# Early heads' x split straight from PSUM, decoding steps moved to other chunks, and the next decoder made ahead of its first step

## The chip, the cores and the metric

The kernel runs on one core of one Trainium2 chip. The time is the device time of one execution in microseconds (us). Kernels are compared by the median of several executions. The engines are TensorE (PE, with its weight loads PEld), VectorE (DVE), ScalarE (ACT), GpSimd (POOL) and SyncE (SP), whose queue issues all DMA transfers of this kernel.

## What is computed

Three stages follow each other: attention with a decay over 4 batches of 8 heads (sequence 576, head width 64), and two feed-forward layers on the 2304 tokens. [...]

```
def _attn_ref(q, k, v, f):                  # (4, 8, 576, 64) each, f (4, 8, 576)
    scores = scale * np.matmul(q, k.transpose(0, 1, 3, 2))
    cum = np.cumsum(np.log(np.clip(f, 0.0001, 1.0)), axis=-1)
    scores = np.where(causal, -1e9, scores + cum[..., :, None] - cum[..., None, :])
    attn = softmax(scores)
    return np.matmul(attn, v)

def _moe_ref(x, w1, w2, w3, w_out):         # x (2304, 512), d_ff 1024
    return ((x @ w1) * (x @ w2) @ w3) @ w_out

def _moe2_ref(x, w_in, w_out, a, b):        # d_ff 2048
    h = x @ w_in
    g = (a0 + a1*h + a2*h*h + a3*h*h*h) / (1 + |b0|*|h| + |b1|*h*h + 1e-6)
    return g @ w_out
```

## The kernel before

Products in the feed-forward layers keep 32-bit accuracy by splitting an operand into a high part (rounded to the matmul's 32-bit format, `...h`) and a low part (the rest, `...l`): high times high, high times low and low times high are three matmuls into one bank.

**The attention loop.** The loop over `t` walks through heads: `n, c = divmod(t, 5)`, so a head `n` has five chunks `c` of up to 128 query rows. There are 32 heads. In chunk `c` of head `n` TensorE transposes the probabilities of the head before (`p_transpose`), makes the scores of the next chunk (`score_mm`, into two banks `ps_s` used in turn), and DVE takes their maximum (`score_max`, line 328), ACT the exponential (`score_exp`, line 339), DVE the reciprocal of the sums (`score_rcp`, lines 347 and 349) and POOL multiplies by it (`score_norm`, line 354). The normalization comes in groups: for heads 0 to 7 in the chunks 3 and 0, from head 8 on in the chunks 2, 4 and 0. Everything is written out in this order by hand, and each engine works its own queue in order.

**Early heads.** Heads 0 to 7 (`n < N32`) multiply by V in plain 32-bit format (`pv_early`, into the bank pair `ps_w`, chunks 2 to 4 of the head after). Two chunks after the last of these, in chunk 0 of head `n + 2`, `pv_out` copies the result of head `n` on DVE from `ps_w` into half of `xr` (line 412); for every second head `x_split` then rounds the pair of heads on ACT into `xh` (line 423) and subtracts on DVE into `xl` (line 425, both inputs in SBUF). Heads from 8 on have `pv` into `ps_v` with split operands, `pv_out` adds two halves (ACT line 414, DVE line 415), and `x_split` subtracts on POOL.

**Loading the next pair of heads.** In an even head the transposes of the next pair's q (chunk 1) and k (end of chunk 2) go into `ps_v` (`qk_transpose`, lines 250 and 251). The transposes of q wait for `pv_out` to have read `ps_v`, those of k for `prep` to have read it (ACT line 258, DVE line 260, in chunks 2 and 3).

**Fillers.** From head 9, chunk 2, TensorE has filler work between the pieces of attention: `gen_ab` multiplies a finished batch by w1 and w2 into the banks `ps_f`, so many ns per chunk (`FILL1`). ACT copies one product to `a_sb` (line 490) and DVE multiplies (line 493). The first filler needs `xh` and `xl` of all of batch 0.

**Decoding.** A `Decoder` turns 64-bit weights into 32 bits, one `step` at a time, four jobs deep: a step's instructions are the low part of job k-3 (line 89, DVE and POOL in turn for w1 and w2), the high part of k-2 (ACT, line 92), an integer add of k-1 (POOL, line 98), shift and mask of job k (DVE, lines 102 and 105) and its low word (ACT, line 108). The transfers are issued ahead on SP (line 68). `gen_w12` has 16 jobs of 512 elements (19 steps); it is followed by `gen_wo2`, which decodes w_out of the second layer in pieces of 256 elements. `side_step` does one step; the loop calls it at the `t` of

```
    DEC_AT = {4, 10, 16, 22, 28, 34, 40}
    ...
        if t == 65:
            while side:
                side_step()
            side.append(gen_wo2())
            side_step()
        if t in DEC_AT or (46 <= t < 65 and t % 2 == 0) or (t > 65 and c in (1, 3)):
            side_step()
```

so at t = 65 (head 13, chunk 0) the last steps of the first decoder, the making of the second one with its transfers, and the second one's first step stand directly behind each other. In the chunk this place lies behind `score_max` and ahead of `prep`, `score_norm` and `pv_out`.

After the attention loop come the rest of `gen_ab`, the product of w3 and w_out, the first layer's second half and the second layer; the change touches none of them.

Of the kernel before, what the change touches and what calls it, by code (L numbers as in the profile page):

```python
# [19 lines left out]
P = 128  # L20
# [100 lines left out]
def kernel(  # L121
# [265 lines left out]
    def pv_early(n, c):  # L387
        r, v = QN[c], vf[(n // 2) % 2]
        for k in range(c + 1):
            t = ptf[:, k, Q0[c] - P : Q0[c] - P + r] if c else ptf0[n % 2]  # L390
            mm(w_ps[0:D, Q0[c] : Q0[c] + r], v[:, k, n % 2, :], t, k == 0, k == c)
# [14 lines left out]
    def pv_out(n):  # L406
        b, h = divmod(n, H)
        hp, j = divmod(h, 2)
        x = xr[hp % 2]
        a, c = slice(64 * j, 64 * (j + 1)), slice(64 * (1 - j), 64 * (2 - j))  # L410
        if n < N32:
            nc.vector.tensor_copy(x[a], w_ps[0:D])
            return
        nc.scalar.copy(xtmp[a], v_ps[c])
        nc.vector.tensor_tensor(out=x[a], in0=v_ps[a], in1=xtmp[a], op=ALU.add)

    def x_split(n):
# [6 lines left out]
        eng = nc.vector if n < N32 else nc.gpsimd  # L424
        eng.tensor_tensor(
# [31 lines left out]
    def gen_wo2():  # L457
# [5 lines left out]
        with pool("d3", "right") as rp:  # L463
            dec_ = Decoder(nc, rp, "d3", PIECE2, 3, 3, jobs)
            while dec_.step():
                yield
# [89 lines left out]
    DEC_AT = {4, 10, 16, 22, 28, 34, 40}  # L556
    FILL1 = [1300.0, 1450.0, 1350.0, 1150.0, 700.0]
    late_x = None
# [3 lines left out]
    for t in range(NCH * (NH + 1) + 2):  # L562
# [25 lines left out]
        if live:  # L588
            score_max(n, c, 0)
        if grp:  # L590
            score_rcp(grp[1], grp[2], 0)
# [9 lines left out]
        if t == 65:  # L601
            while side:
                side_step()
            side.append(gen_wo2())
            side_step()
        if t in DEC_AT or (46 <= t < 65 and t % 2 == 0) or (t > 65 and c in (1, 3)):
            side_step()
# [19 lines left out]
        if c == 0 and 0 <= n - 2 < NH:  # L627
            pv_out(n - 2)
            if n - 1 == N32:
                psw.close()  # L630
                psf = ps1.enter_context(
                    tc.tile_pool(name="psf", bufs=1, space=PSUM, reuse_waits="tile")
                )
                ps_f += [psf.tile([P, 512], F32, name=f"ps_f{i}") for i in range(2)]
        if c == 1 and n % 2 == 1 and 0 <= n - 2 < NH and n not in (H + 3, H + 5):
            x_split(n - 2)
        if n == H + 5 and c == 0:
            x_split(H + 1)
        if n == H + 5 and c == 3:
# [350 lines left out]
```

## Time and profile before

| | |
|---|---|
| median of 3 executions | 1031.2 us (1029.83 to 1032.1) |
| the profiled execution | 1027.81 us, its span 1026.0 us |
| PE busy | 985.7 us, 96% of the span |
| PEld busy | 898.1 us, 88% |
| DVE busy | 794.6 us, 77% |
| ACT busy | 673.9 us, 66% |
| POOL busy | 383.3 us, 37% |

The span is what lies between the first and the last instruction; the 1.8 us beside it are the execution's own. An engine is busy while one of its instructions is being carried out, and for PE the ends of the matmuls are modelled. In the timeline a row shows the start, the duration, the engine, the line, the operation with output and inputs, and in square brackets how long the engine sat idle ahead of it and what ended that wait. [...]

### The profile page before, as it was taken

To read this page: it belongs to the slowest core of one execution; us is meant where nothing else is said; L and a number is where in the kernel's file an instruction comes from. 1 tells how busy PE (TensorE), PEld (TensorE's weight loads), DVE (VectorE), ACT (ScalarE), POOL (GpSimd) and SP (SyncE) were. 2 spreads that over 40 slices of the span, in tenths; PEclk is the share of its full clock that TensorE was granted. 3 is DMA by queue.
4 is the path that set the end of the run, shared out by engine and by line. 5 is a ranking of instruction groups with operands and counts; after the bars stand their busy time and mean duration, and the time that the engine had idled before them with its cause. 6 is when DMAs were issued, how large, how long until landed. Compare 5 with 4: busy or idle time off the path is not lost.

```text
span 1026.0 us, 18623 instructions
## 1 busy us (share of the span) xinstructions
PE 985.7 (96%) x6224; PEld 898.1 (88%) x6224; DVE 794.6 (77%) x1799; ACT 673.9 (66%) x1542; POOL 383.3 (37%) x476
## 2 busy tenths in 40 slices
PE   6888888999999999999999999999999999999998
PEld 4666788999999999998899998899999888899997
DVE  5787886777777765788988637888888888888886
ACT  5666665666666664445566537777777777777775
POOL 7445565444444432453455401222222222222221
PEclk9999998999999999999999999999999999999999
DMA  5868465666666530665579741010010100100000
GB/s 130 216 161 180 132 154 153 179 176 178 177 180 180 152 81 30 205 204 182 178 225 302 232 139 37 1 32 32 1 62 1 31 32 1 32 32 1 32 1 32
DMA packets 126352, 114.98 MB, mean 112 GB/s; under 512 B 65456, under 2 KB 94640, under 8 KB 126256
## 3 DMA queue, kind: packets, MB, share of 16 engines
q1 hardware_dynamic: 126256, 113.79, 39.6%
q8 instruction: 49, 0.80, 0.3%
q14 instruction: 47, 0.39, 0.1%
HBM read 70.61 MB, written 23.22 MB: 91 GB/s over the span
## 4 chain that ended last, share of the span: by engine, by line
PE 84%; DVE 4%; DMA 2%; issue 2%; ACT 2%; SPq 0%; POOL 0%; DVEq 0%; POOLq 0%; ACTq 0%
PE bank L160 47%; PE ps_f L160 19%; PE ps_v L160 6%; PE ps_s L160 5%; PE ps_x L359 4%; PE ps_v L250 1%; PE ps_w L160 1%; DVE pr L328 1%; DVE d_f L102 1%; DMA d_r<-in_moe_w_in_dram 1%; PE ps_v L251 0%; DMA z_dr<-z_sb 0%; DMA d_r<-in_moe_w_dram 0%; DVE cl L433 0%; DMA d_r<-in_moe_w_out_dram 0%
## 5 line engine op out<-in xcount | busy, mean ns | idle before, releaser
L887 POOL TENSOR_TENSOR gl<-pp,gh 128x384 fp32r<-128x384 f32 x96 | 97.7, 1017 | 320.8 <-PE bank L160 267.0
L354 POOL TENSOR_SCALAR pr<-pr,st 128x128 f32<-128x128 f32 (+4 forms) x160 | 93.9, 598 | 176.2 <-DVE st L349 66.2
L328 DVE CUSTOM_DVE_ANT_0 pr<-ps_s,mask 128x128 f32<-128x128 f32 (+4 forms) x160 | 83.0, 522 | 68.3 <-PE ps_s L160 63.5
L160 PE MATMUL bank<-ch,wih 128*128 128x384 f32 x384 | 129.1, 336 | 2.0 <-DVE pp L908 2.0
L160 PE MATMUL bank<-ch,wil 128*128 128x384 f32 x384 | 129.4, 337 | 0.0
L160 PE MATMUL bank<-cl,wih 128*128 128x384 f32 x384 | 128.6, 335 | 0.0
L339 ACT ACTIVATE pr<-pr,st 128x128 f32<-128x128 f32 (+4 forms) x160 | 97.1, 607 | 32.2 <-DVE st L328 31.8
L160 PE MATMUL bank<-wo2h,gl 128*128 128x512 f32 x288 | 113.9, 395 | 0.0
L160 PE MATMUL bank<-wo2h,gh 128*128 128x512 f32 x288 | 113.5, 394 | 0.0
L160 PE MATMUL bank<-wo2l,gh 128*128 128x512 f32 x288 | 113.5, 394 | 0.0
L98 POOL TENSOR_TENSOR d_f<-d_f,d_r 128x256 int32<-128x256 int32 (+1 forms) x96 | 87.8, 915 | 45.1 <-DVE d_f L105 18.6
L894 ACT ACTIVATE h<-bank 128x384 f32<-128x384 f32 x96 | 47.0, 490 | 86.9 <-PE bank L160 86.1
L383 ACT CAST pth<-ps_x 128x256 fp32r<-128x256 f32 (+1 forms) x96 | 44.4, 462 | 61.2 <-PE ps_x L359 40.5
L160 PE MATMUL ps_s<-kh,qs 128*128 128x128 f32 (+2 forms) x192 | 76.0, 396 | 8.6 <-DVE st L328 5.2
L160 PE MATMUL bank<-cl,w3oh 128*128 128x256 f32 x288 | 80.8, 281 | 0.9 <-DVE cl L433 0.9
L160 PE MATMUL bank<-ch,w3ol 128*128 128x256 f32 x288 | 80.7, 280 | 0.5 <-DVE w3ol L777 0.5
L359 PE MATMUL ps_x<-ident,pr 128*128 128x128 f32 (+1 forms) x480 | 75.7, 267 | 5.5 <-POOL pr L354 2.8
L160 PE MATMUL bank<-ch,w3oh 128*128 128x256 f32 x288 | 80.6, 280 | 0.0
L160 PEld LDWEIGHTS bank<-ch,wih 128*128 128x128 f32 x384 | 72.0, 188 | 6.9 <-DVE pp L908 2.7
L911 DVE SCALAR_TENSOR_TENSOR qv<-qv,rr 128x384 f32<-128x384 f32 x96 | 53.7, 559 | 31.3 <-ACT rr L906 31.3
L108 ACT ACTIVATE d_r<-d_r 128x256 int32<-128x256 uint32 (+1 forms) x128 | 59.9, 471 | 26.7 <-DMA d_r<-in_moe_w_dram 13.8
L901 DVE SCALAR_TENSOR_TENSOR qv<-h,pb_abs,qv 128x384 f32<-128x384 f32 x96 | 59.1, 616 | 23.1 <-ACT qv L895 23.1
(167 smaller groups left out, 3053.6 us busy)
## 6 DMA issues: line engine op xcount, KB each, us to landing
d_r<-in_moe_w_out_dram SPq DMA_DIRECT2D x48, 256.0 KB
c_dr<-c_sb SPq DMA_DIRECT2D x64, 144.0 KB
cl<-c_dr SPq DMA_DIRECT2D x36, 256.0 KB
d_r<-in_moe_w_dram SPq DMA_DIRECT2D x16, 512.0 KB
d_r<-in_moe_w_dram SPq DMA_DIRECT2D x32, 256.0 KB
d_r<-in_moe_w_in_dram SPq DMA_DIRECT2D x32, 256.0 KB
kh<-kh SPq DMA_DIRECT2D x45, 144.0 KB
z_dr<-z_sb SPq DMA_DIRECT2D x36, 128.0 KB
```

The lines of the kernel that those rows point to most:

```text
L98: nc.gpsimd.tensor_tensor(out=u, in0=u, in1=r[:, :, 0], op=ALU.add)
L108: nc.scalar.activation(low, low.bitcast(U32), AF.Copy, scale=2.0**-29)
L160: nc.tensor.matmul(o, lhsT, rhs, start=start, stop=stop)
L328: nc.vector.tensor_tensor_reduce(out=pr[0:r, OFF[c] + a : OFF[c] + b], in0=ps_s[(t + part) % 2][0:r, 0 : b - a], in1=mask[0:r, 512 - Q0[c] ...
L339: nc.scalar.activation(x, x, AF.Exp, bias=st[0:r, 0, c : c + 1], scale=-1.0, accum_out=st[0:r, 1, c : c + 1],)
L354: nc.gpsimd.tensor_scalar(x, x, st[0:r, 1, c : c + 1], 1.0, op0=ALU.mult, op1=ALU.mult)
L359: nc.tensor.transpose(ps_x[x][:, r * j : r * (j + 1)], pr[0:r, o + P * j : o + P * (j + 1)], ident[0:r, 0:r],)
L383: nc.scalar.copy(hi, src)
L887: nc.gpsimd.tensor_tensor(out=at(gl, j), in0=at(pp, j), in1=raw(at(gh, j)), op=ALU.subtract)
L894: nc.scalar.activation(at(h2, i), h, AF.Square)
L901: nc.vector.scalar_tensor_tensor(out=at(qv, i), in0=at(h2, i), scalar=pb_abs[:, 1:2], in1=at(qv, i), op0=ALU.mult, op1=ALU.add,)
L911: nc.vector.scalar_tensor_tensor(out=at(qv, i), in0=at(qv, i), scalar=QC, in1=at(rr, i), op0=ALU.add, op1=ALU.mult)
```

## The change

Four things are changed.

- `pv_early` writes the rows of `ps_w` that belong to the head's half (0 to 63 or 64 to 127). `pv_out` rounds them for early heads on ACT straight into `xh`, and a new function `x_low` subtracts on DVE, from PSUM, into `xl`, in chunk 1 of head `n + 2`, directly behind that chunk's `score_max`. `xr`, the copy on DVE and the early heads' `x_split` fall away.
- The decoding steps of `gen_w12` stand at other `t`: 7, 12, 17, ... 42 (all chunk 2), 44, 46, 48 and then chunks 1 and 3 up to 68.
- `gen_wo2` yields once behind its making, so that it is made at t = 69 (head 13, chunk 4) and takes its first step at t = 71.
- `x_split` for heads 8 and 9 moves from t = 65 to t = 69, for heads 10 and 11 from head 13 to head 14, chunk 3. The banks `ps_f` are taken over a chunk later.

```diff
--- before.py
+++ after.py
@@ -388,7 +388,7 @@
         r, v = QN[c], vf[(n // 2) % 2]
         for k in range(c + 1):
             t = ptf[:, k, Q0[c] - P : Q0[c] - P + r] if c else ptf0[n % 2]
-            mm(w_ps[0:D, Q0[c] : Q0[c] + r], v[:, k, n % 2, :], t, k == 0, k == c)
+            mm(w_ps[HALF[n % 2], Q0[c] : Q0[c] + r], v[:, k, n % 2, :], t, k == 0, k == c)
 
     def pv(n):
         i, j = (n // 2) % 2, n % 2
@@ -409,10 +409,17 @@
         x = xr[hp % 2]
         a, c = slice(64 * j, 64 * (j + 1)), slice(64 * (1 - j), 64 * (2 - j))
         if n < N32:
-            nc.vector.tensor_copy(x[a], w_ps[0:D])
+            nc.scalar.copy(xh[0][a, hp], w_ps[a])
             return
         nc.scalar.copy(xtmp[a], v_ps[c])
         nc.vector.tensor_tensor(out=x[a], in0=v_ps[a], in1=xtmp[a], op=ALU.add)
+
+    def x_low(n):
+        hp, j = divmod(n % H, 2)
+        r = HALF[j]
+        nc.vector.tensor_tensor(
+            out=xl[0][r, hp], in0=w_ps[r], in1=raw(xh[0][r, hp]), op=ALU.subtract
+        )
 
     def x_split(n):
         b, h = divmod(n, H)
@@ -421,8 +428,7 @@
             side_step()
         x = xr[hp % 2]
         nc.scalar.copy(xh[b % 2][:, hp], x)
-        eng = nc.vector if n < N32 else nc.gpsimd
-        eng.tensor_tensor(
+        nc.gpsimd.tensor_tensor(
             out=xl[b % 2][:, hp], in0=x, in1=raw(xh[b % 2][:, hp]), op=ALU.subtract
         )
 
@@ -462,6 +468,7 @@
                 jobs.append((w_out2[P * j : P * (j + 1), cs], None, None, None, wo2_dr[j, :, cs]))
         with pool("d3", "right") as rp:
             dec_ = Decoder(nc, rp, "d3", PIECE2, 3, 3, jobs)
+            yield
             while dec_.step():
                 yield
 
@@ -553,8 +560,9 @@
     nc.gpsimd.memset(st, 1.0)
 
     NPAIR = NH // 2
-    DEC_AT = {4, 10, 16, 22, 28, 34, 40}
+    DEC_AT = {*range(7, 43, 5), 44, 46, 48, 51, 53, 56, 58, 61, 63, 66, 68}
     FILL1 = [1300.0, 1450.0, 1350.0, 1150.0, 700.0]
+    T_X1 = NCH * (H + 5) + 4
     late_x = None
     pt = []
     late = ExitStack()
@@ -587,6 +595,8 @@
             score_exp((c - 1) % NCH)
         if live:
             score_max(n, c, 0)
+        if c == 1 and 0 <= n - 2 < N32:
+            x_low(n - 2)
         if grp:
             score_rcp(grp[1], grp[2], 0)
         if late_x is not None:
@@ -598,12 +608,11 @@
         flush()
         if t == 10:
             w12["dec"].ahead = 4
-        if t == 65:
-            while side:
-                side_step()
+        if t == T_X1:
+            x_split(H + 1)
             side.append(gen_wo2())
             side_step()
-        if t in DEC_AT or (46 <= t < 65 and t % 2 == 0) or (t > 65 and c in (1, 3)):
+        if t in DEC_AT or (t > T_X1 and c in (1, 3)):
             side_step()
         if t == 0:
             first_q(1)
@@ -626,17 +635,15 @@
             late_x = (m, cc)
         if c == 0 and 0 <= n - 2 < NH:
             pv_out(n - 2)
-            if n - 1 == N32:
-                psw.close()
-                psf = ps1.enter_context(
-                    tc.tile_pool(name="psf", bufs=1, space=PSUM, reuse_waits="tile")
-                )
-                ps_f += [psf.tile([P, 512], F32, name=f"ps_f{i}") for i in range(2)]
-        if c == 1 and n % 2 == 1 and 0 <= n - 2 < NH and n not in (H + 3, H + 5):
+        if c == 1 and n - 1 == N32:
+            psw.close()
+            psf = ps1.enter_context(
+                tc.tile_pool(name="psf", bufs=1, space=PSUM, reuse_waits="tile")
+            )
+            ps_f += [psf.tile([P, 512], F32, name=f"ps_f{i}") for i in range(2)]
+        if c == 1 and n % 2 == 1 and N32 <= n - 2 < NH and n not in (H + 3, H + 5):
             x_split(n - 2)
-        if n == H + 5 and c == 0:
-            x_split(H + 1)
-        if n == H + 5 and c == 3:
+        if n == H + 6 and c == 3:
             x_split(H + 3)
         if c == 4 and n % 2 == 0 and N32 <= n < NH:
             split_v(p)
```

The order in which the instructions stand shows this at three places. On DVE, in head 2, chunks 0 to 2 (`ps_w` holds the result of head 0, `xr_136` the copied half, `xl_101` the low part, `d_f` and `d_r` the decoder's tiles, `ps_s` the scores, `ps_v` the next pair's q). Before:

```order
L349 RECIPROCAL st<-st 128x2
L102 TENSOR_SCALAR d_f_170<-d_r_166 128x512
L105 SCALAR_TENSOR_TENSOR d_f_170<-d_r_166,d_f_170 128x512
L412 COPY xr_136<-ps_w 64x576
L328 ISA pr,st<-ps_s_84,mask 128x256
L328 ISA st 128x1
L328 ISA pr,st<-ps_s_83,mask 128x384
L328 ISA st 128x1
L260 SCALAR_TENSOR_TENSOR qs_113<-ps_v,qs_112 128x576
```

and in the changed kernel:

```order
L349 RECIPROCAL st<-st 128x2
L328 ISA pr,st<-ps_s_84,mask 128x256
L328 ISA st 128x1
L420 TENSOR_TENSOR xl_101<-ps_w,xh_100 64x576
L328 ISA pr,st<-ps_s_83,mask 128x384
L328 ISA st 128x1
L102 TENSOR_SCALAR d_f_170<-d_r_166 128x512
L105 SCALAR_TENSOR_TENSOR d_f_170<-d_r_166,d_f_170 128x512
L260 SCALAR_TENSOR_TENSOR qs_113<-ps_v,qs_112 128x576
```

The decoding step moved from ahead of the maximum of chunk 1 to between the maximum of chunk 2 and `prep` of q (line 260). On DVE, in head 10, chunks 0 and 1, where line 415 is what the transposes of q wait for (`c_sb` is a filler's product). Before:

```order
L349 RECIPROCAL st<-st 128x1
L493 TENSOR_TENSOR c_sb_104<-ps_f_1072,a_sb_102 128x288
L89 TENSOR_TENSOR w2l<-d_f_171,w2h 128x2x256
L102 TENSOR_SCALAR d_f_170<-d_r_166 128x512
L105 SCALAR_TENSOR_TENSOR d_f_170<-d_r_166,d_f_170 128x512
L415 TENSOR_TENSOR xr_136<-ps_v,xtmp 64x576
L328 ISA pr,st<-ps_s_84,mask 128x256
```

and in the changed kernel:

```order
L349 RECIPROCAL st<-st 128x1
L500 TENSOR_TENSOR c_sb_104<-ps_f_1107,a_sb_102 128x288
L415 TENSOR_TENSOR xr_136<-ps_v,xtmp 64x576
L328 ISA pr,st<-ps_s_84,mask 128x256
L328 ISA st 128x1
L385 TENSOR_TENSOR ptl<-ps_x_85,pth 128x2x128
L89 TENSOR_TENSOR w1l<-d_f_169,w1h 128x2x256
L102 TENSOR_SCALAR d_f_172<-d_r_168 128x512
L105 SCALAR_TENSOR_TENSOR d_f_172<-d_r_168,d_f_172 128x512
```

The step's three instructions moved from ahead of line 415 to behind the maximum of chunk 1. On ACT, in head 13, chunk 0, around the second decoder's first low word (`d_r_1707`, a tile that a transfer of w_out fills). Before:

```order
L339 ACTIVATE pr,st<-pr,st 64x576
L92 CAST w2h<-d_f_172 128x2x256
L108 ACTIVATE d_r_1707<-d_r_1707 128x256
L383 CAST pth<-ps_x_86 128x2x128
L414 COPY xtmp<-ps_v 64x576
L423 CAST xh_1702<-xr_136 128x576
L339 ACTIVATE pr,st<-pr,st 128x128
L490 COPY a_sb_103<-ps_f_1071 128x288
```

and in the changed kernel, from head 13, chunk 4, to head 14, chunk 1 (`d_r_1808` is the same tile of the second decoder):

```order
L339 ACTIVATE pr,st<-pr,st 128x512
L430 CAST xh_1801<-xr_136 128x576
L383 CAST pt0h_133<-ps_x_86 128x128
L339 ACTIVATE pr,st<-pr,st 64x576
L383 CAST pth<-ps_x_85 128x2x128
L414 COPY xtmp<-ps_v 64x576
L339 ACTIVATE pr,st<-pr,st 128x128
L497 COPY a_sb_103<-ps_f_1106 128x288
L108 ACTIVATE d_r_1808<-d_r_1808 128x256
```

The first low word moved two chunks behind the making of its decoder, and in head 13, chunk 0, nothing that a transfer fills stands ahead of the filler's copy any more.

## Rows read from the trace of the kernel before

**Rows 1.** Busy time by stretch: start:end, length, each engine's busy us (instructions), PEclk, DMA.
```profile
18.00:97.00 79.00, 67.31 (x504) 52.11 (x504) 58.90 (x177) 51.96 (x141) 35.59 (x56) 1.00 0.77 180
97.00:171.00 74.00, 61.37 (x404) 56.20 (x403) 60.17 (x156) 45.60 (x116) 44.20 (x47) 0.91 0.60 156
171.00:400.00 229.00, 229.00 (x1699) 216.89 (x1698) 160.19 (x555) 149.91 (x398) 102.01 (x142) 1.00 0.58 152
105.70:109.00 3.30, 3.30 (x16) 3.24 (x15) 3.27 (x4) 1.77 (x6) 2.64 (x2) 0.50 0.19 41
146.60:150.00 3.40, 3.40 (x16) 3.29 (x16) 1.93 (x5) 1.45 (x4) 2.06 (x3) 0.50 0.08 26
163.70:170.40 6.70, 5.54 (x23) 5.05 (x24) 6.31 (x17) 4.09 (x13) 3.69 (x5) 0.50 0.46 126
```

**Rows 2.** Timeline of PE from 97 to 171 us: start, duration, instruction, idle ahead.
```profile
103.64 0.40 PE L160 MATMUL ps_f<-xl,w1h 128*128 128x288 f32 x1 [1.54 <-DVE xl L425]
...
116.97 0.65 PE L250 MATMUL ps_v<-ident,q_raw 128*128 128x128 f32 x4 [2.73 <-DVE xr L415]
...
145.27 0.66 PE L250 MATMUL ps_v<-ident,q_raw 128*128 128x128 f32 x4 [1.60 <-DVE xr L415]
...
164.86 0.61 PE L160 MATMUL ps_f<-xh,w1h 128*128 128x288 f32 x1 [3.44 <-ACT a_sb L490]
```

**Rows 3.** Timeline of ACT in head 13, chunk 0.
```profile
162.08 0.44 ACT L108 ACTIVATE d_r<-d_r 128x256 int32<-128x256 uint32 x1 [5.18 <-DMA d_r<-in_moe_w_out_dram]
```

**Rows 4.** Timeline of DVE and PE in head 16, chunks 1 and 2, and head 18, chunk 2.
```profile
203.22 0.28 DVE L102 TENSOR_SCALAR d_f<-d_r 128x256 int32<-128x256 int32 x1
203.53 0.43 DVE L105 SCALAR_TENSOR_TENSOR d_f<-d_r,d_f 128x256 int32<-128x256 int32 x1
...
205.45 0.75 DVE L260 SCALAR_TENSOR_TENSOR qs<-ps_v,qs 128x576 fp32r<-128x576 f32 x1
...
207.62 0.60 PE L250 MATMUL ps_v<-ident,k_raw 128*128 128x128 f32 x4
...
230.41 0.75 DVE L260 SCALAR_TENSOR_TENSOR qs<-ps_v,qs 128x576 fp32r<-128x576 f32 x1
```

**Rows 5.** Timeline of DVE in head 4, chunk 2, with a decoding step.
```profile
51.37 2.04 DVE L89 TENSOR_TENSOR w1l<-d_f,w1h 128x512 fp32r<-128x512 f32 x1
...
54.41 0.75 DVE L260 SCALAR_TENSOR_TENSOR qs<-ps_v,qs 128x576 fp32r<-128x576 f32 x1
```

**Rows 6.** Timeline of POOL at the same place.
```profile
51.55 1.30 POOL L98 TENSOR_TENSOR d_f<-d_f,d_r 128x512 int32<-128x512 int32 x1
```

**Rows 7.** Timeline of PE in the early heads: the waits for DVE.
```profile
33.72 0.50 PE L160 MATMUL ps_s<-kh,qs 128*128 128x512 f32 x1 [0.82 <-DVE st L328]
...
46.05 0.45 PE L160 MATMUL ps_s<-kh,qs 128*64 128x512 f32 x1 [1.10 <-DVE st L328]
...
55.21 0.66 PE L250 MATMUL ps_v<-ident,k_raw 128*128 128x128 f32 x4 [1.64 <-DVE qs L260]
...
65.58 0.45 PE L160 MATMUL ps_s<-kh,qs 128*64 128x512 f32 x1 [1.27 <-DVE st L328]
...
79.72 0.44 PE L160 MATMUL ps_s<-kh,qs 128*128 128x384 f32 x1 [0.63 <-DVE st L328]
...
90.61 0.50 PE L160 MATMUL ps_s<-kh,qs 128*128 128x512 f32 x1 [0.89 <-DVE st L328]
```

**Rows 8.** Instructions by line: count, duration in ns (min/median/max), first and last start, form.
```profile
L412 DVE COPY xr<-ps_w x8: 729/746/751, 32.6 to 98.0; 64x576 f32<-64x576 f32 x8
...
L425 POOL TENSOR_TENSOR xl<-xr,xh x12: 1415/1428/1435, 164.3 to 409.7; 128x576 fp32r<-128x576 f32 x12
L425 DVE TENSOR_TENSOR xl<-xr,xh x4: 750/754/3189, 44.8 to 102.8; 128x576 fp32r<-128x576 f32 x4
...
L415 DVE TENSOR_TENSOR xr<-ps_v,xtmp x23: 740/751/764, 116.2 to 399.1; 64x576 f32<-64x576 f32 x23
...
L414 ACT COPY xtmp<-ps_v x24: 631/636/639, 112.6 to 407.5; 64x576 f32<-64x576 f32 x24
```

## The prediction

> **What bounds the kernel now.** I read the busy time by stretch first, to see where TensorE (PE) is not the bound. From 171 us to 400 us PE is busy for the whole 229.00 us at the full clock, so nothing that the other engines do there can save time; after that the change alters nothing. Ahead of it are two stretches with room [rows 1]. In the early heads, 18 to 97 us, PE is busy 67.31 of 79.00 us, 11.69 us idle, with the clock at 1.00 throughout. In heads 9 to 13, 97 to 171 us, fillers are there to keep PE busy, and still 12.63 us are idle and the granted clock is 0.91: three stretches at 0.50 (1.2 GHz) hold 3.30, 3.40 and 5.54 us of busy PE [rows 1]. Work that takes x at half clock takes about x/2 at full clock, so these cost (3.30 + 3.40 + 5.54) / 2 = 6.1 us. All that the change can give is therefore 11.7 us of idle in the early heads, 12.6 us in heads 9 to 13, and 6.1 us of clock.
>
> Next I read the timeline of PE for what ended its waits. Four waits make 9.31 of the 12.63 us in heads 9 to 13: 1.54 us for the last low part of x, 2.73 and 1.60 us for `pv_out` (line 415) ahead of the transposes of q in heads 10 and 12, and 3.44 us for a filler's copy on ACT [rows 2]. The last one has its reason on ACT: in head 13, chunk 0, it stood still for 5.18 us for the first transfer of the second decoder, with that copy queued behind [rows 3]. In the early heads, six waits of 0.63 to 1.64 us end with a DVE instruction [rows 7]; five of them are a score matmul waiting for its bank.
>
> **The change part by part.** *The second decoder.* The first low word now stands two chunks behind the transfers that it needs; ACT's wait was 5.18 us and two chunks last about as long (`prep` of q came at 205.45 us in head 16 and at 230.41 us in head 18 [rows 4], ten chunks in 24.96 us, 2.5 us each), so the wait is hidden, apart from a tenth or so of it. The 3.44 us go, and with them the stretch at half clock that begins at the end of that wait (2.8 us). What is late next is head 14: `x_split` of heads 8 and 9 now runs on POOL (1.43 us [rows 8]) one chunk ahead of `pv_out` of head 12, which overwrites the same `xr` and so has to wait for it on DVE, with the maxima queued behind it and PE's transposes of q waiting for it. That costs between 0 and 1.4 us. I take 0.4, near the lower end, since a chunk lies between. Steps of the second decoder that come later lie in the stretch in which PE is never idle.
>
> *The first filler.* The 1.54 us for the low part of x go: `x_low` of head 7 stands ahead of the decoding step on DVE, not behind it, and the ACT rounding is done a chunk earlier. The later take-over of the banks `ps_f` costs nothing, since the first filler comes a chunk later still.
>
> *Steps of heads 10 and 12.* They move from chunks 0, 2 and 4 to chunks 1 and 3, so `pv_out` no longer stands behind three decoding instructions: the 2.73 and 1.60 us go. What is late next is `prep` of q in chunk 2, for which the transposes of k wait. In head 16, where steps already stand in chunks 1 and 3, `prep` ended at 206.20 us and PE came at 207.62 us, a slack of 1.42 us, with a step of 203.22 to 203.96, 0.74 us, ahead of it [rows 4]. The steps moved here are of 512 elements; the one in head 4 kept DVE from 51.37 to 54.41, 3.04 us [rows 5]. So the new wait is at most 3.04 - 0.74 - 1.42 = 0.9 us and at least none; I take 0.5 in each of the two heads, the middle, as half of the steps have no DVE subtraction. Together 2.73 + 1.60 - 1.0 = 3.3 us.
>
> *The clock.* The falls at 105.7 and 146.6 us come behind the waits of 1.54 and 1.60 us, the third one behind the 3.44 us [rows 1, 2]. With these waits gone I expect none of the three: 6.1 us.
>
> Sum of heads 9 to 13: 1.54 + 3.44 + 3.3 - 0.4 + 6.1 = 14.0 us. Its ends are 8.9 us (1.54 + 3.44 + 4.33 - 1.8 - 1.4, and the third fall alone, 2.8) and 18.7 us (all of 12.63 and 6.1).
>
> *Early heads, x.* DVE loses eight copies (0.75 us each) and four subtractions, one of which lasted 3.19 us against a median of 0.75, and gains eight of `x_low`; line 415 is of the same kind, with one input in PSUM, and lasted 0.740 to 0.764 us in 23 instances [rows 8]. ACT loses four casts and gains eight of about 0.64 us (line 414 [rows 8]); it is not what PE waits for here, so I put this at nothing, between 0 and the 8 x 0.64 us. [...]
>
> The two halves of `ps_w` buy nothing: the changed kernel's first `pv_early` matmul of a head waits for the `x_low` just made, of the other half, because the bank is tracked as one. It has been read behind the maximum of chunk 1, and a score matmul stands in front on PE, so I count this wait as hidden, too; its upper bound is 0.75 us per head.
>
> *Early heads, steps.* Moving the steps takes away five waits: 0.82 + 1.10 + 1.27 + 0.63 + 0.89 = 4.7 us [rows 7]. But four of the new places, in heads 2, 4, 6 and 8, lie directly ahead of `prep` of q, and the kernel before has one step there, in head 4. It cost PE 1.64 us [rows 7]: DVE's subtraction took 2.04 us from 51.37 us on, with POOL's add of the same step, 1.30 us, beginning at 51.55 us [rows 5, 6]. It is the step's own add that held it, in a chunk without a group of normalization, so the new places do not keep DVE from being held. I take 1.64 us for heads 6 and 8 and 1.2 for head 2, whose step has no subtraction, so 4.5 us; the wait in head 4 stays. In the odd heads the step lies ahead of the maximum of chunk 3; bounds are 0 and the 1.27 us of the wait behind the long subtraction [rows 7], and I take 0.5 for three of them, as PE has the rest of `pv_early` to do meanwhile. The early heads then lose 4.5 + 1.5 - 4.7 = 1.3 us, between a gain of 4.7 and a loss of 4.5 + 3.8 - 4.7 = 3.6.
>
> [...]
>
> **How the numbers follow.** 14.0 - 1.3 = 12.7 us. The profiled execution took 1027.81 us, so it would be 1015.1; it was 3.4 us quicker than the median of the runs, 1031.2, and I set the sum against that: 1018.5 us. A measurement can tell about 0.2%, 2 us, from no change. The base case has a chance of 0.53.
>
> **Rivals.** *More (0.14).* The five smaller waits of heads 9 to 13, 12.63 - 9.31 = 3.3 us, are DVE being late behind decoding and go as steps get rarer (two per head for three); the 1.0 and 0.4 us do not appear, and the early heads come out 2 us better than even: 14.0 + 3.3 + 1.4 + 2.0 = 20.7, so 1010.5 us.
>
> *DVE becomes the bound (0.16).* It was already busy 60.17 of 74.00 us there [rows 1], and steps held by POOL stay long. Heads 10 and 12 wait the full 0.9 us (0.8 more), two of the three falls remain (3.3), and each of five heads loses 0.7 us elsewhere (3.5): 12.7 - 7.6 = 5.1, so 1026.1 us. For it speaks that hardly a fifth of DVE's time is free; against it, that head 11 already has its steps in chunks 1 and 3 and none of the four large waits.
>
> *The second decoder does not come early enough (0.06).* SP issues in order, and if a store ahead holds its transfers, the 3.44 and 2.8 us stay: 1024.7 us. Against it speaks that they were issued and landed within the 5.18 us.
>
> *Slower (0.06): the early heads lose the clock.* They keep PE just 85% busy, and two falls came behind waits no longer than the 1.64 us that would now come four times. Each stretch of 3.4 us at half clock costs 1.7 us; eight of them are 13.6, and eight full waits for `x_low` 6.0: 12.7 - 19.6, so 1038 us. It decides from the point where both exceed 14.7 us, for instance six falls with six waits. Against it speaks that the clock stayed at 1.00 through the one wait of 1.64 us.
>
> *No change (0.05):* the two middle rivals together, 1029 to 1033 us.
>
> Faster by more than 0.2%: 0.53 + 0.14 + 0.16 + 0.06 = 0.89; within it 0.05; slower 0.06. The range, 1009.5 to 1027, spans the base case but for its ends and most of the first three rivals.
>
> **What would show it.** PE's idle time from 97 us to the end of head 13 should fall from 12.6 to about 5 us and the clock there be 1.00; no wait of ACT for a transfer of w_out above 1 us. The early heads should show waits for line 260 of 1.2 to 1.7 us in heads 2, 4, 6 and 8, and no wait of `pv_early` for `x_low` above 0.2 us. The forecast is wrong if the falls of the clock come elsewhere, or if PE's idle time in the early heads moves by more than 4 us.

## The result and the profile after

| | before | after |
|---|---|---|
| median, measured side by side | 1031.38 us (1029.83 to 1032.1) | 1018.28 us (1016.53 to 1018.97) |
| the profiled execution, its span | 1027.81 us, 1026.0 us | 1016.53 us, 1014.7 us |

The changed kernel takes 0.9879 of the time before, 95% interval 0.9863 to 0.9896: 13.1 us less between the medians, 11.3 us less between the two profiled executions. The forecast was 1018.5 us, in a range of 1009.5 to 1027.

Where the time came from is read best between three moments that both kernels have: the start of the first exponential (line 339, 128x128) of heads 9, 10 and 14. Before, these stand at 97.6, 113.1 and 176.8 us; after, at 102.5, 115.4 and 166.5 us. The busy time between these moments follows, for the kernel before and then for the changed one; columns as in [rows 1]. PEclk is the clock granted to PE as a share of full speed: in the kernel before, the fillers' matmuls of 288 columns start 0.13 us apart at 1.00 (171.27 to 172.19 us) and 0.24 us apart at 0.50 (105.74 to 107.90 us). The first spacing is 0.55 of the second, where the prediction takes x/2; the second is 1.2 columns per ns, the nearest that the traces come to the prediction's 1.2 GHz, from which nothing is worked out.

```profile
18.00:97.60 79.60, 67.81 (x506) 52.40 (x505) 59.28 (x181) 52.56 (x143) 36.20 (x57) 1.00 0.77 180
97.60:113.10 15.50, 12.05 (x74) 10.94 (x75) 13.71 (x35) 9.64 (x25) 10.05 (x12) 0.89 0.70 175
113.10:176.80 63.70, 54.62 (x371) 50.66 (x370) 49.20 (x133) 38.90 (x98) 36.53 (x39) 0.92 0.56 146
```

```profile
18.00:102.50 84.50, 70.82 (x510) 55.13 (x510) 62.51 (x187) 58.39 (x153) 41.71 (x61) 0.96 0.70 178
102.50:115.40 12.90, 9.88 (x72) 8.89 (x71) 11.53 (x28) 8.17 (x21) 7.41 (x10) 1.00 0.95 230
115.40:166.50 51.10, 49.99 (x372) 47.16 (x370) 40.07 (x122) 36.20 (x93) 28.62 (x34) 1.00 0.58 150
171.00:400.00 229.00, 229.00 (x1703) 217.38 (x1702) 159.32 (x543) 148.10 (x391) 101.77 (x140) 1.00 0.57 153
```

The same 371 and 372 matmuls of heads 10 to 13 take 51.1 us instead of 63.7: PE idles 1.1 us instead of 9.1, at full clock instead of 0.92. That is 12.6 us. Up to the start of head 10 the changed kernel is 2.3 us late; up to head 9 even 4.9, of which 1.9 us are idle time and 3.0 us busy time, for its two stretches at half clock now lie ahead of head 9 where the first one used to lie behind it. From 171 us on PE is busy throughout in both [rows 1].

The waits of PE that are left in the early heads, and the two stretches at half clock:

```profile
35.70 0.66 PE L250 MATMUL ps_v<-ident,k_raw 128*128 128x128 f32 x4 [1.49 <-DVE qs L260]
48.96 0.30 PE L160 MATMUL ps_s<-kh,qs 128*128 128x128 f32 x1 [1.47 <-DMA kh<-kh]
55.33 0.66 PE L250 MATMUL ps_v<-ident,k_raw 128*128 128x128 f32 x4 [1.63 <-DVE qs L260]
67.09 0.33 PE L359 MATMUL ps_x<-ident,pr 128*128 128x128 f32 x1 [1.03 <-POOL pr L354]
74.55 0.66 PE L250 MATMUL ps_v<-ident,k_raw 128*128 128x128 f32 x4 [1.43 <-DVE qs L260]
87.64 0.33 PE L359 MATMUL ps_x<-ident,pr 128*128 128x128 f32 x1 [1.03 <-POOL pr L354]
95.35 0.66 PE L250 MATMUL ps_v<-ident,k_raw 128*128 128x128 f32 x4 [1.89 <-DVE qs L260]
```

```profile
76.10:79.40 3.30, 3.30 (x17) 2.64 (x17) 2.04 (x6) 1.04 (x4) 0.85 (x2) 0.50 0.82 238
96.60:99.90 3.30, 3.30 (x14) 2.15 (x13) 2.00 (x6) 2.14 (x6) 1.60 (x3) 0.50 0.51 156
```

The four waits for line 260 (heads 2, 4, 6, 8) were forecast, and two in the odd heads, which end here with POOL's multiply behind the late maximum; the wait for `kh<-kh`, a transfer that stacks k for head 4, and the two stretches at 0.50 were not. SP's queue shows why that transfer is late (start, duration of the issue, what is moved, how often):

```profile
33.80 1.46 SPq L68 DMA_DIRECT2D d_r<-in_moe_w_dram  x3
35.76 1.15 SPq L304 DMA_DIRECT2D qb<-qs  x2
42.44 0.46 SPq L304 DMA_DIRECT2D qs<-qs  x1
```

At t = 10 the decoder's prefetch becomes four jobs deep, and the next step, now in head 2, chunk 2, issues three transfers of 512 KB at once, directly ahead of the first stacking transfer. The next one of the chain is issued 5.5 us later (35.76 + 1.15 to 42.44), as if each had to land behind the weights. The kernel before issues the same three transfers, but from the step in chunk 0 of that head, and there the two links of the chain lie 4.1 us apart (35.84 + 1.15 to 41.12):

```profile
31.64 2.37 SPq L68 DMA_DIRECT2D d_r<-in_moe_w_dram  x3
35.84 1.15 SPq L304 DMA_DIRECT2D qb<-qs  x2
41.12 0.46 SPq L304 DMA_DIRECT2D qs<-qs  x1
```

### The profile page after: what moved, and what is told of

It reads as the page before. It is cut to its first block, busy times and chain, and to the rows that moved or that the text cites. A ratio compares the mean times of both kernels' runs of the same rounds, so it can differ in the third digit from the quotient of the medians.

```text
span 1014.7 us, 18627 instructions
## 1 busy us (share of the span) xinstructions
PE 979.4 (97%) x6224; PEld 892.6 (88%) x6224; DVE 787.5 (78%) x1795; ACT 676.6 (67%) x1546; POOL 382.0 (38%) x476
## 4 chain that ended last, share of the span: by engine, by line
PE 83%; DVE 6%; DMA 3%; issue 3%; ACT 2%; POOL 2%; SPq 0%; POOLq 0%; ACTq 0%; DVEq 0%
PE bank L160 47%; PE ps_f L160 18%; PE ps_v L160 6%; PE ps_s L160 5%; PE ps_x L359 4%; PE ps_v L250 1%; DVE d_f L102 1%; DMA d_r<-in_moe_w_dram 1%; DVE pr L328 1%; DMA kh<-kh 1%; PE ps_w L160 1%; DVE cl L439 1%; DMA z_dr<-z_sb 1%; DMA d_r<-in_moe_w_in_dram 0%; PE ps_v L251 0%
## 5 line engine op out<-in xcount | busy, mean ns | idle before, releaser
L354 POOL TENSOR_SCALAR pr<-pr,st 128x128 f32<-128x128 f32 (+4 forms) x160 | 91.5, 584 | 172.7 <-DVE st L349 65.3
L160 PEld LDWEIGHTS bank<-cl,wih 128*128 128x128 f32 x384 | 72.1, 188 | 4.3
```

The lines of the kernel that those rows point to most:

```text
L160: nc.tensor.matmul(o, lhsT, rhs, start=start, stop=stop)
L354: nc.gpsimd.tensor_scalar(x, x, st[0:r, 1, c : c + 1], 1.0, op0=ALU.mult, op1=ALU.mult)
```

## The experiments

Twelve kernels were run; ratios are to the kernel before, measured beside them. Head 9, 10 and 14 are the starts of their first exponentials in the profiled execution, in us; none of the twelve leaves anything out of the computation. These columns come from one execution each, and differences of a us or two in them show nothing: second decoder only has the instructions of the kernel before up to t = 64, and no yield those of the changed kernel up to t = 69, and yet their heads 9 and 10 start 1.0 to 2.1 us later.

| kernel | median us | ratio (95%) | head 9 | head 10 | head 14 |
|---|---|---|---|---|---|
| before | 1031.38 | | 97.6 | 113.1 | 176.8 |
| x only | 1029.54 | 0.9973 to 1.0008 | 101.7 | 115.7 | 179.6 |
| second decoder only | 1023.57 | 0.9902 to 0.9954 | 98.7 | 114.1 | 174.4 |
| all but x | 1021.97 | 0.9907 to 0.9955 | 103.8 | 119.3 | 170.3 |
| changed kernel | 1018.28 | 0.9863 to 0.9896 | 102.5 | 115.4 | 166.5 |
| changed, early steps of before | 1016.75 | 0.9844 to 0.9894 | 100.1 | 115.8 | 167.6 |
| changed, no yield | 1018.1 | 0.9874 to 0.9910 | 104.6 | 116.7 | 167.7 |
| changed, prep first | 1017.25 | 0.9866 to 0.9895 | 103.5 | 117.0 | 168.0 |
| changed, deep from t = 45 | 1016.86 | 0.9845 to 0.9893 | 103.3 | 116.4 | 167.4 |
| changed, add later | 1016.2 | 0.9839 to 0.9894 | 99.7 | 114.1 | 165.0 |
| prep first, deep from t = 45 | 1017.77 | 0.9843 to 0.9900 | 98.5 | 114.6 | 165.6 |
| prep first, deep from t = 35 | 1013.74 | 0.9823 to 0.9870 | 99.7 | 113.3 | 164.3 |
| add later, deep from t = 35 | 1014.24 | 0.9821 to 0.9867 | 97.8 | 111.0 | 162.0 |
| all three | 1012.34 | 0.9804 to 0.9852 | 97.3 | 111.2 | 162.2 |

In the three kernels with the add later, line numbers behind the decoder are 5 higher (265 for 260, 165 for 160), and the step's subtraction is line 90 for 89.

### Which part gives the gain

**x only:** the kernel before with `pv_early`'s halves, `x_low` and the later take-over of `ps_f`; steps and second decoder as before.

```diff
-            nc.vector.tensor_copy(x[a], w_ps[0:D])
+            nc.scalar.copy(xh[0][a, hp], w_ps[a])
...
+        if c == 1 and 0 <= n - 2 < N32:
+            x_low(n - 2)
```

> The kernel before with the x part alone: early heads' x from PSUM (pv_early into the head's half, rounding on ACT, x_low on DVE), steps and second decoder where they were before. My theory: the x part takes away the 1.54 us wait of the first filler and the fall of the clock behind it (1.7 us), and in the early heads the part of the waits at 46.05 and 65.58 us that the long subtraction made (1 to 2 us); the waits of 2.73, 1.60 and 3.44 us stay. About 1027 us against 1031.2, between 1025.5 and 1029. Rival: the x part is worth nothing, since the first filler then waits for the next late thing on DVE: 1030 to 1032 us. The wait of pv_early for x_low stays under 0.2 us in either.

1029.54 us: no change. The waits that x was to remove are gone (the 1.27 and 1.54 us of [rows 7] and [rows 2]). Of the five waits in [rows 7] that the prediction has the steps take away, 4.7 us, only 0.53 and 0.62 us are left, the first two of these rows; others of PE stand in their place:

```profile
45.72 0.45 PE L160 MATMUL ps_s<-kh,qs 128*64 128x512 f32 x1 [0.53 <-DVE st L328]
79.32 0.44 PE L160 MATMUL ps_s<-kh,qs 128*128 128x384 f32 x1 [0.62 <-ACT xh L412]
50.14 0.30 PE L160 MATMUL ps_s<-kh,qs 128*128 128x128 f32 x1 [1.58 <-DMA kh<-kh]
88.55 0.44 PE L160 MATMUL ps_s<-kh,qs 128*128 128x128 f32 x1 [2.33 <-issue]
107.32 0.49 PE L359 MATMUL ps_x<-ident,pr 64*128 64x64 f32 x5 [1.74 <-DVE st L349]
```

The first matmul with a new `kh` is the first use of a new pair of heads; its "issue" wait at 88.55, without a releaser in the records, stands at the same point of head 8.

**Second decoder only:** made at t = 69, with its yield, and the first decoder's last two steps at t = 66 and 68 instead of in one go at t = 65.

```diff
+            yield
...
-        if t == 65:
-            while side:
-                side_step()
+        if t == T_X1:
+            x_split(H + 1)
```

> The kernel before with the second decoder alone changed: it is made in head 13, chunk 4, with its first step two chunks later, and the first decoder's last steps follow in chunks 1 and 3 up to t = 68; the steps ahead of that and the early heads' x stay as before. Nothing is left out. Theory (each of the parts brings its own waits): ACT's 5.18 us and PE's 3.44 us in head 13 go, with the stretch at half clock there (2.8 us): 6 us less than the kernel before, 1024 to 1026 us, while the waits of 1.54, 2.73 and 1.60 us in heads 9, 10 and 12 stay. Rival (the idle time goes to the next wait, as it did when x alone was changed): the 3.44 us are replaced by waits for line 415 or 260 in heads 13 and 14, less than 2 us gained, 1028 to 1031 us.

1023.57 us, ratio 0.9928: the theory by its time, and half a us better. Heads 10 to 13 take 60.3 us for 63.7 in the profiled execution, at 1026.48 us the slowest of five. The stretch at half clock in head 13 is gone, but one as long came behind the larger of the waits for line 415, which stay; the first low word no longer waits:

```profile
118.01 1.12 PE L250 MATMUL ps_v<-ident,q_raw 128*128 128x128 f32 x4 [2.72 <-DVE xr L415]
```

```profile
117.50:124.20 6.70, 6.19 (x24) 5.54 (x25) 3.99 (x13) 2.88 (x7) 2.19 (x4) 0.50 0.09 28
```

```profile
175.25 0.44 ACT L108 ACTIVATE d_r<-d_r 128x256 int32<-128x256 uint32 x1
```

**No yield:** the changed kernel without the `yield` in `gen_wo2`, so that its first step follows its making at once.

> The changed kernel with one difference: the second decoder's first step directly behind its making, at t = 69, as before. My theory: ACT and DVE wait for the first transfer again, 3 to 5 us, with the filler's copy behind; PE waits about 3 us, and if the clock falls, 2 to 3 us more: 1021.5 to 1024.5 us against 1018.3. Rival: the wait was made by the two steps drained right ahead of it at t = 65, not by the missing chunk; then 1018 to 1019 us.

1018.1 us, as the changed kernel. ACT waits there once, and PE not at all:

```profile
164.69 0.45 ACT L108 ACTIVATE d_r<-d_r 128x256 int32<-128x256 uint32 x1 [1.32 <-DMA d_r<-in_moe_w_out_dram]
```

So it is not the yield of two chunks that removed most of the 5.18 us [rows 3], as the prediction put it, but the place: in chunk 4, with no last steps of the first decoder in front, the wait is 1.32 us and nobody waits for it. Whether the chunk or the missing steps do it, no run separates.

**All but x:** the kernel before with all of the changed kernel's steps and its second decoder; against the changed kernel, x goes back:

```diff
-            nc.scalar.copy(xh[0][a, hp], w_ps[a])
+            nc.vector.tensor_copy(x[a], w_ps[0:D])
...
-        nc.gpsimd.tensor_tensor(
+        eng = nc.vector if n < N32 else nc.gpsimd
+        eng.tensor_tensor(
```

> The kernel before with the steps of both decoders as in the changed kernel (the second one made in head 13, chunk 4), while the early heads' x stays as before (a copy on DVE to xr, rounding on ACT, subtraction on DVE). Nothing is left out. Theory (x is worth nothing by itself, as e1_x_only showed, and e8_dec_only's 6.5 us came from the second decoder alone): 2.73 and 1.60 us go, 1016 to 1020 us, as the changed kernel within 2 us. Rival (x makes room on DVE once the steps are in their new places): DVE's copies and x_split delay head 2's to 9's maxima, the first filler's wait for xl stays at 1.5 us or more, 1021 to 1025 us.

1021.97 us: the rival. Heads 10 to 13 take 51.0 us, as in the changed kernel, but head 10 starts 3.9 us later. It differs from second decoder only in the steps of the first decoder alone, and the two waits for line 415 (2.72 and 1.59 us there) are gone: the steps' new places removed them. Its PE still waits for the early maxima behind `x_split` (by 1.27 us at 88.16 us, too), and in the first filler:

```profile
67.81 0.45 PE L160 MATMUL ps_s<-kh,qs 128*64 128x512 f32 x1 [1.27 <-DVE st L328]
109.87 0.40 PE L160 MATMUL ps_f<-xl,w1h 128*128 128x288 f32 x1 [1.66 <-DVE xl L425]
```

DVE, same kernel, beside the first of these:

```profile
64.08 3.20 DVE L425 TENSOR_TENSOR xl<-xr,xh 128x576 fp32r<-128x576 f32 x1 [0.27 <-ACT xh L423]
```

So x by itself gives nothing, and 3.7 us between the medians (1021.97 to 1018.28) once the steps have moved; the two intervals of the table do not overlap. The early steps by themselves cost: with the second decoder alone head 10 starts at 114.1 us, with all steps at 119.3.

### What holds up the early heads

**Early steps of before:** the changed kernel with the steps up to t = 40 in their old places.

```diff
-    DEC_AT = {*range(7, 43, 5), 44, 46, 48, 51, 53, 56, 58, 61, 63, 66, 68}
+    DEC_AT = {4, 10, 16, 22, 28, 34, 40, 44, 46, 48, 51, 53, 56, 58, 61, 63, 66, 68}
```

> The changed kernel with the early steps (up to t = 40) where they were before, 4, 10, 16, 22, 28, 34, 40; the later steps, x part and second decoder as changed. My theory: the early moves cost time: head 9 came at 97.6 us before and at 102.5 us in the changed kernel; with the old places it comes at 96 to 98 us and the clock does not fall there: 1012 to 1015 us against 1018.3. Rival: the x part makes the early heads slower, not the places of the steps: 1017 to 1020 us.

1016.75 us (1012.57 to 1018.06): between theory and rival; moving the early steps gained nothing that can be measured. Only one wait for line 260 is left (1.62 us), but head 8 starts late:

```profile
88.14 0.44 PE L160 MATMUL ps_s<-kh,qs 128*128 128x128 f32 x1 [4.58 <-issue]
```

and on SP a weight transfer stands ahead of the last two stacking transfers for that head:

```profile
79.99 0.56 SPq L68 DMA_DIRECT2D d_r<-in_moe_w_dram  x1
80.64 0.46 SPq L304 DMA_DIRECT2D qs<-qb  x1
81.19 0.55 SPq L315 DMA_DIRECT2D kh<-kh  x1
```

**Prep first:** in even early heads `prep` of q ahead of the decoding step.

```diff
-        if t in DEC_AT or (t > T_X1 and c in (1, 3)):
+        step_now = t in DEC_AT or (t > T_X1 and c in (1, 3))
+        if step_now and not (even and c == 2):
             side_step()
...
             prep(p + 1, c - 2, 1)
+        if step_now and even and c == 2:
+            side_step()
```

> The changed kernel with one difference: in even heads the decoding step of chunk 2 is issued behind prep of q, not ahead of it. My theory: the four waits of 1.49, 1.63, 1.43 and 1.89 us for line 260 (6.4 us together) go, and with them the falls of the clock at 76 and 97 us (3.3 us): about 1009 us against 1018.3, between 1007 and 1012. Rival: DVE is late in any case, the step then delays the maximum of chunk 3 and PE waits there for the same time: 1016 to 1019 us.

1017.25 us, no gain over the changed kernel. All waits for line 260 went, 6.4 us together, and one nearly as long came:

```profile
52.03 0.45 PE L160 MATMUL ps_s<-kh,qs 128*128 128x128 f32 x1 [5.39 <-DMA kh<-kh]
```

```profile
34.08 2.34 SPq L68 DMA_DIRECT2D d_r<-in_moe_w_dram  x3
37.05 2.64 SPq L304 DMA_DIRECT2D qb<-qs  x2
45.48 0.46 SPq L304 DMA_DIRECT2D qs<-qs  x1
```

The theory fell: DVE being held is not the only thing that paces the early heads. The three weight transfers are again ahead of the chain, so the runs that follow went to the transfers and the add.

**Deep from t = 45:** the prefetch stays two jobs deep in the early heads.

```diff
-        if t == 10:
+        if t == 45:
             w12["dec"].ahead = 4
```

> The changed kernel with the decoder's prefetch left two jobs deep until t = 45 (for four jobs deep from t = 10). Nothing is left out. Theory (the early heads lose their time to stacking transfers that stand behind a burst of three 512 KB weight transfers issued in head 2): the 1.47 us wait of PE for kh at 47.5 us goes, and with it the later start of heads 5 to 8; head 9 starts at about 100 us (102.5 in the changed kernel), the time is 1015 to 1017 us. The four waits for line 260 stay. Rival (the burst does not matter, since the waits for line 260 pace the early heads): head 9 starts at 102 to 103 us, 1017.5 to 1019 us. Rival on the other side: with two jobs deep a step waits on DVE for its transfer by more than 1 us, head 9 starts behind 104 us, over 1020 us.

1016.86 us. The wait for `kh` went, as the first theory said, and with one weight transfer ahead of them the two links of the chain lie 2.8 us apart (36.80 + 1.15 to 40.75, for 5.5); but head 9 is no earlier: the step in head 2 now waits for its own weights, which is the third case, in one place only.

```profile
37.62 0.66 PE L250 MATMUL ps_v<-ident,k_raw 128*128 128x128 f32 x4 [3.11 <-DVE qs L260]
```

```profile
35.58 0.43 DVE L102 TENSOR_SCALAR d_f<-d_r 128x512 int32<-128x512 int32 x1 [2.89 <-DMA d_r<-in_moe_w_dram]
```

**Add later:** POOL's add of an early step two chunks after the step.

```diff
+        if t - 2 in DEC_AT and t < 43 and c == 4:
+            w12["dec"].add(w12["dec"].at - 1)
```

> The changed kernel with POOL's integer add of a step (line 98) issued two chunks later in the early heads, in chunk 4 of the same head, away from the step's own work on DVE. Nothing is left out. Theory (the step's own add holds DVE): the subtractions of line 89 in heads 4, 6 and 8 shrink from 1.7 to 2.0 us to about 0.7, the waits for line 260 in heads 4, 6 and 8 fall by about 1.2 us each; head 9 starts 1.5 to 3.6 us earlier, at 99 to 101 us, and the time is 1015 to 1017 us. Rival (DVE is held by other work on POOL, and the waits stay): subtractions unchanged, head 9 at 102 to 103 us, 1018 us. Second rival (the waits go, but the stacking transfers end last, as when prep stood ahead of the step): waits for line 260 below 0.6 us, a wait of PE for kh of over 3 us in their place, 1017 to 1018.5 us.

1016.2 us, with head 9 at 99.7: the theory by its numbers, but by the waits partly the second rival. The subtractions of the early heads, by line with their mean, in the changed kernel and with the add later:

```profile
L89 DVE TENSOR_TENSOR w1l<-d_f,w1h 128x512 fp32r<-128x512 f32 x2 | 2.4, 1206 | 0.0
L89 DVE TENSOR_TENSOR w2l<-d_f,w2h 128x512 fp32r<-128x512 f32 x1 | 1.7, 1743 | 0.0
```

```profile
L90 DVE TENSOR_TENSOR w1l<-d_f,w1h 128x512 fp32r<-128x512 f32 x2 | 1.4, 679 | 0.0
L90 DVE TENSOR_TENSOR w2l<-d_f,w2h 128x512 fp32r<-128x512 f32 x1 | 0.7, 680 | 0.0
```

So the step's own add does hold DVE, as [rows 5] and [rows 6] suggested, and 0.68 us is the price without it. The waits for line 260 in heads 4, 6 and 8 fell from 1.63, 1.43 and 1.89 to none, 0.66 and 0.96 us, that of head 2, 1.79 us, stayed, and the two of the odd heads went. In return the waits for `kh` grew, to 3.39 us and, in head 8, 1.34 us:

```profile
51.00 0.30 PE L165 MATMUL ps_s<-kh,qs 128*128 128x128 f32 x1 [3.39 <-DMA kh<-kh]
```

**Prep first, deep from t = 45:** the two edits together.

> Both: in even early heads prep of q ahead of the step (as in e2_prep_first), and the prefetch two jobs deep until t = 45 (as in e5_ahead_later). Nothing is left out. Theory (waits for line 260 and transfers behind the weights are the only two things that pace the early heads): neither a wait for line 260 above 0.5 us nor one for kh above 1 us, no stretch of PE at half clock ahead of 100 us; head 9 starts at 95 to 98 us and the time is 1009 to 1013 us. Rival (the transfers of the weights and of q and k share the DMA engines whatever their order, so the waits for kh only move): waits for kh of over 2 us stay in heads 4 to 8, head 9 at 100 us or later, 1015 to 1018 us.

1017.77 us. Both kinds of wait went, and head 9 starts at 98.5 us; but head 10 is at 114.6. In head 9, with a step every two chunks, two jobs are too few, and ACT waits for the weights, with PE behind it (2.38 us at 106.39 us, for line 349):

```profile
103.91 0.68 ACT L108 ACTIVATE d_r<-d_r 128x512 int32<-128x512 uint32 x1 [4.42 <-DMA d_r<-in_moe_w_dram]
```

**Prep first, deep from t = 35:** the three transfers now go out in head 7, where no stacking follows.

> As e7_prep_ahead, but the prefetch becomes four jobs deep at t = 35 (in force from the step at t = 37, head 7, chunk 2) and not at t = 45. Nothing is left out. Theory (what took the early heads' gain in e7_prep_ahead was the weights' coming late: ACT waited 4.42 us and DVE 3.68 us for d_r in head 9, chunk 1): these waits go below 1 us, PE's wait of 2.38 us at 104 us goes below 1 us, head 10 starts at 110 to 112 us (114.6 there), the time is 1011 to 1014 us. Rival (what is gained up to head 9 is lost to stretches at half clock in heads 8 to 10, whatever the waits): head 10 starts at 113 us or later, 1015 to 1018 us. Rival on the other side: the burst in head 7 holds up the stacking transfers for head 8, a wait of PE for kh of over 2 us there, 1016 to 1019 us.

1013.74 us. ACT's waits are gone (the same instruction, at 100.61 us, waits for nothing) and so is PE's of 2.38 us; the time is the theory's, though its interval still overlaps that of prep first, deep from t = 45. Head 10, at 113.3 us, is the rival's: in this execution PE ran at half clock from 98.8 to 105.6 us.

```profile
100.61 0.68 ACT L108 ACTIVATE d_r<-d_r 128x512 int32<-128x512 uint32 x1
```

**Add later, deep from t = 35**, and **all three**:

> As e6_add_later (POOL's integer add two chunks later), and the prefetch four jobs deep from t = 35. Nothing is left out. Theory (with the adds away the early heads only wait for kh behind the weights): the waits for kh of 3.39, 0.72 and 1.34 us go, one wait for line 260 in head 2 of about 3 us comes (its step waits for its transfer, as in e5_ahead_later), head 10 starts at 110 to 113 us, the time is 1012 to 1015 us. Rival: waits for kh stay since every step still issues one weight transfer ahead of the stacking, head 10 at 114 us, 1016 us as e6_add_later.

1014.24 us: no wait for `kh` is left, head 10 starts at 111.0 us, as the theory has it. But line 265 is waited for in four heads and not in one: by 1.45, 2.51, 0.65 and 1.41 us, the longest behind a step whose line 100 waited 1.68 us for its weights, so two jobs are too few in head 4 as well.

> All three: prep of q ahead of the step, the integer add two chunks later, the prefetch four jobs deep from t = 35. Nothing is left out. Theory (the waits are separate and add): no wait for line 260 above 0.5 us, none for kh above 1 us, DVE's subtractions in the early heads at 0.7 us; head 9 at 96 to 98 us, head 10 at 109 to 111 us, 1010 to 1013 us. Rival (once prep is ahead of the step, DVE's being held costs nothing more): as e9_prep_depth within 1.5 us.

1012.34 us, with an interval (0.9804 to 0.9852) that lies below the changed kernel's: some 6 us better, and the best of these kernels. Whether the add later gains anything on top of prep first isn't settled by 1.4 us, which the rival has, too. Its stages, up to heads 9, 10 and 14:

```profile
18.00:97.30 79.30, 68.06 (x506) 53.65 (x507) 56.52 (x185) 57.50 (x152) 40.25 (x61) 0.98 0.71 182
97.30:111.20 13.90, 11.81 (x74) 10.71 (x75) 12.49 (x30) 8.30 (x22) 9.01 (x10) 0.88 0.88 202
111.20:162.20 51.00, 49.90 (x372) 47.08 (x370) 39.77 (x122) 36.15 (x92) 28.53 (x33) 1.00 0.65 165
```

## Why the prediction was right, and where it was not

**Heads 9 to 13: right in cause, a little low.** From head 10 to 14 the terms of the sum were 2.73 + 1.60 - 1.0 + 3.44 - 0.4, and 1.7 + 2.8 for the stretches at 146.6 and 163.7 us: 10.9 us. Measured are 12.6. The 1.0 us for the transposes of k and the 0.4 for `x_split` didn't appear at all; that is 1.4 of the missing 1.7. The waits for line 415 go with the steps and the 3.44 us with the second decoder, as the runs of the parts show. The first low word of the second decoder came without a wait:

```profile
167.28 0.44 ACT L108 ACTIVATE d_r<-d_r 128x256 int32<-128x256 uint32 x1
```

From head 9 to 14 PE idled 4.1 us (3.0 and 1.1 by the windows; about 5 were forecast), and the clock stayed at 1.00: of the three stretches none came once the waits were gone. The rivals that put a new bound on DVE or a late second decoder there are out.

**The second decoder: right in size, wrong in reason.** The run without the yield shows that its place (with no last steps in front), not its two chunks, takes PE's wait away.

**Early heads: the step that failed.** For the part up to head 10 the sum had a gain of 1.9 us (1.54 + 1.7 for the stretch at 105.7 us, less 1.3); measured is a loss of 2.3 (and of 2.6 between the two kernels that repeat these instructions, second decoder only and no yield). In head 9 itself 2.6 us were gained of 3.2, nearly all of it by the clock: PE's idle time fell from 3.4 to 3.0 us only, for when the first filler's 1.54 us had gone, the wait for line 349 grew from 0.71 to 1.23 us and one of 0.87 us for line 385 came. Ahead of head 9 the sum had a loss of 1.3 us, and 4.9 were measured. The waits that I priced came as priced: those for line 260 are 6.4 us in all, against 4.5 + 1.64, and the odd heads' two are 2.1, against 1.5. What failed is the clock and the transfers. I gave the early heads no fall of the clock, since it had stayed at 1.00 through one wait of 1.64 us; it fell twice (1.65 us each), and I had thought of that only as the slower rival, with eight falls. And of the moved steps I counted the DVE work, not the weight transfers that they issue on SP: the wait for `kh` of 1.47 us. Together these are 4.8 us, somewhat more than the 4.2 by which the sum was off here. I had named two signs of being wrong. The first, falls of the clock elsewhere, came true, so for the early heads the forecast is wrong by its own measure. The second, idle time in the early heads that moves by more than 4 us, did not: between 18 us and head 9 it went from 11.8 to 13.7 us, and the rest of that loss is clock.

**x: right alone, wrong in company.** I put its part at nothing and gave the steps the credit for all five waits taken away. Without x two waits of 1.27 us and the first filler's stay, and 3.7 us are lost; with x alone, the steps in their old places, just 0.53 and 0.62 us of the five are left. So most of the credit belonged to x, and the early moves, once x is there, had about 1.2 us of waits to take away and brought those for line 260. Line 420 cost what line 415 had suggested, and PE never waited for it; the roundings on ACT (line 412) took 0.64 us each. By line, the eight subtractions from PSUM, mean in ns:

```profile
L420 DVE TENSOR_TENSOR xl<-ps_w,xh 64x576 fp32r<-64x576 f32 x8 | 6.0, 755 | 1.4 <-ACT xh L412 1.4
```

**The total.** 12.7 us were forecast; the profiled executions differ by 11.3 (10.3 of it by head 14), the medians by 13.1. The sum of the parts was thus 1.4 us too high, and that the point came within 0.3 us is luck: heads 10 to 13 gave more than forecast and the early heads lost more, and the gap between the profile of before and the median made up the rest. Measured against the quicker profile of before, it would have been 1015.1, with 1016.5 found.

**Open:** what sets the falls of the clock in the early heads. They come in other places in every kernel, also where no wait above 1.2 us is left: with prep first and the prefetch deep from t = 45 the clock was at half from 96.6 to 103.4 us. Nor do they keep their places from one execution to another: no yield, with the changed kernel's instructions up to t = 69, had them from 51.8 to 55.2 and from 96.2 to 103.0 us. No run held everything else still and changed PE's idle time alone.

## What to carry to other kernels

A step that is moved takes its transfers along: look at what stands behind them in the issuing queue, above all small transfers on which a later stage waits (in the changed kernel the wait for `kh` of 1.47 us), and raise a prefetch's depth in a place where nothing urgent follows (1013.74 us from t = 35, for 1017.77 from t = 45). Where several late things end at nearly the same moment, removing one shows the next: here DVE's held steps, the stacking transfers and the weights each had to go before the time moved, and single edits measured as nothing (x alone, 0.9973 to 1.0008 of the time before; prep alone, 1017.25 us, and depth alone, 1016.86, for the changed kernel's 1018.28). Judge such a change by stages between fixed points of the program, and from more than one execution, not by its total alone, or gains and losses of several us hide each other.

## What the hardware showed that I had not expected

A VectorE instruction of two columns was held beside one on POOL, like a big one. In head 8 of the changed kernel line 347 took 1.09 us beside POOL's add, against 0.17 us in head 6 with nothing on POOL beside it (DVE, then POOL):

```profile
68.97 0.17 DVE L347 TENSOR_SCALAR st<-st 128x2 f32<-128x2 f32 x1
91.68 1.09 DVE L347 TENSOR_SCALAR st<-st 128x2 f32<-128x2 f32 x1
```

```profile
91.45 1.29 POOL L98 TENSOR_TENSOR d_f<-d_f,d_r 128x512 int32<-128x512 int32 x1
```

It ends, at 92.77 us, just when the add does (92.74). The subtractions of line 89 agree: 1.74 us at 71.02 us, beside an add from 70.91 to 72.21 us, but 0.67 us at 92.89 us, with the add over, and 0.68 us with the add later. They have two inputs and line 347 has one; what decides whether DVE is held, no run separates.

Small transfers behind large ones are the other thing: with three transfers of 512 KB directly ahead, 5.5 us (changed kernel) and 5.8 us (prep first, 37.05 + 2.64 to 45.48) lay between two links of a chain of 144 KB transfers, with one ahead 2.8 us (deep from t = 45) and 3.8 us (prep first, deep from t = 45, 34.33 + 1.14 to 39.28).
